# Attention scores as plain float32 products on two row tiles of TensorE, and token mixing through one difference

## The chip, the core and the metric

The kernel runs on one core of a Trainium2 chip. A core has five engines with instruction streams of their own: TensorE (PE in the profile; its weight loads are the row PEld), VectorE (DVE), ScalarE (ACT), GpSimd (POOL) and SyncE (SP, which here only issues DMA transfers). Matrix products are written to PSUM, all else lies in SBUF, and inputs and outputs in HBM. The metric is the device time of one execution in microseconds (us), as the median of several runs.

## The reference

Two layers behind one another: attention with a distance bias over a short local window and a few global keys, then a channel mix ("k" and "r" branches) on its output.

```python
# q, k, v: (4, 8, 768, 64) float32; n_global = 8, n_local = 96
scores = q @ k.T / 8
keep = is_global | is_local            # key < 8, or 0 <= query - key < 96
dist = where(is_global & ~is_local, n_local, abs(query - key))
scores = where(keep, scores - slope[h] * dist, -1e9)
a = exp(scores - max); a = a / (sum(a) + 1e-9)
x = (a @ v), heads side by side        # (4, 768, 512)

x_prev = x shifted by one token, zeros first
xk = mu_k * x + (1 - mu_k) * x_prev
xr = mu_r * x + (1 - mu_r) * x_prev
k = maximum(xk @ w_k, 0)               # (512, 1024)
v = (k * k) @ w_v                      # (1024, 512)
out = sigmoid(xr @ w_r) * v
```

The weights arrive as float64, everything else as float32.

## The kernel before

**Tiles and chunks.** The 4 x 768 tokens are 24 tiles of 128 queries (6 to a batch) and 12 chunks of 256 tokens (two tiles). A tile sees at most 256 keys: 32 from the start of the batch, the 96 before the tile, and its own 128; a batch's first tile (0, 6, 12, 18) has only its own 128.

**Attention of a tile**, for each pair of heads `hp`: `scores` multiplies q and k on PE into one of two PSUM banks `s`; DVE adds the bias (`pat`, or `pat0` for a batch's first tile), takes the row maximum `nmax` and writes `e` (L295); ACT takes exp and the row sum (L296); for every four heads DVE makes the reciprocal `r` (L302, L303) and POOL scales `e` with it (L306). A tile later `transposes` turns `e` on PE (L317) and ACT copies it to `et` (L318); another tile later `weighted` multiplies with `v` into `av` (L334), two heads on two halves of PE's columns, and ACT copies `av` to the chunk's `x` (L345).

**Score products.** A head has 64 rows, PE's array 128. The first `NATIVE` = 7 tiles use plain float32 (L287) with q and k padded by 64 rows of zeros: the two buffers `qz` and `kz` are zeroed once by POOL (L205, L206). From tile 7 on, `load_tile` brings q and k twice, to the upper and the lower 64 partitions, and `split_tile` makes float32r operands of them, that is, rounded values and remainders: `qh` and `kw` by POOL (L196 is the line of its copy helper), `ql` and the lower half of `kw` by DVE (L265, L266), and the keys before the tile by POOL from the previous tile's `kw`. A head is then two float32r products (L289, L290).

**Weights.** Twenty pieces of 128x512 are converted from float64 on the fly during the first tiles: ACT and POOL or DVE shift the exponent (L166 to L170), DVE puts the bits together (L171 to L173), ACT or POOL rounds to the high part (`wk_hi`, `wr_hi`, `wv_hi`, L174 or L196), POOL subtracts to get the low part (`wk_lo`, `wr_lo`, `wv_lo`, L180).

**Channel mix of a chunk**: `mix` makes xk and xr. Of each four column blocks, POOL (for chunk 0 ACT) multiplies x_prev by 1 - mu (L357, L355), DVE adds mu * x (L358), ACT rounds to the high part (L359) and DVE subtracts to get the low part (L360). Then `three` does each product as three float32r products (L371 to L373) into `kp` (first layer), `z` (the gate) and `vps` (second layer); DVE and ACT square `kp` (L397 to L400) and form `sig` (L414), SP stores the result.

**Order.** The loop over 24 steps weaves the pieces: at step n the loads of tile n+1, `weighted` of tile n-2, `transposes` of tile n-1, `scores` of tile n, and between them slices of the channel mix of an earlier chunk (`run_ffn`), and the conversion of weights (`weights_go`). A scheduler then fixes each engine's order before the run; each engine works through its own in order.

Of the kernel before, what the change touches and what calls it, by code (L numbers as in the profile page):

```python
# [24 lines left out]
NATIVE = 7  # first tiles, whose scores are plain float32 products  # L25
# [4 lines left out]
HUGE = (1.875 - 2.0**-13) * 2.0**32  # bits 0x4FEFFC00  # L30
# [3 lines left out]
def tile_biased_attention_channel_mix(ctx: ExitStack, tc: tile.TileContext, qT, kT, v, n_sizes, mu_kr, w_k, w_v, w_r, q_rows, k_rows, v_rows, slopes, out):  # L34
# [33 lines left out]
    kw_pool = fast.enter_context(tc.tile_pool(name="kw", bufs=2))  # L68
    q_pool = fast.enter_context(tc.tile_pool(name="qp", bufs=2))
# [7 lines left out]
    ps_s = fast.enter_context(tc.tile_pool(name="ps_s", bufs=2, space=PSUM))  # L77
# [4 lines left out]
    # the tensor engine's clock rises with use: products of zeros until the first tile is there  # L82
# [7 lines left out]
    # The distance; n_local for a key that is only global, which is over any distance of a local key;  # L90
    # FAR or more where masked: such a key's weight is exactly 0.
# [13 lines left out]
    # 96 keys before the tile, then the tile's own  # L105
# [9 lines left out]
    # tile 0  # L115
# [11 lines left out]
    # later tiles: 32 keys from the start, 96 keys before the tile, the tile  # L127
# [10 lines left out]
    pool.tensor_scalar(mus1, mus, -1.0, 1.0, op0=ALU.mult, op1=ALU.add)  # L138
# [60 lines left out]
    state = {}  # L199
    # the first tiles' queries and keys, with 64 rows of zeros: products of all 128 rows keep the tensor engine's clock up  # L200
    padded = []
    for i in range(2):
        qz = q_pool.tile([128, H, 128], F32, name=f"qz_{i}", tag="qh")
        kz = kw_pool.tile([128, H, 256], F32, name=f"kz_{i}", tag="kw")
        pool.memset(qz[64:128], 0.0)  # L205
        pool.memset(kz[64:128], 0.0)  # L206
        padded.append((qz, kz))

    def load_tile(n):
        b, t = divmod(n, NT)  # L210
        s = state[n] = {}
        native = n < NATIVE
        halves = (0,) if native else (0, 64)
        if native:
            qr, kr = padded[n % 2]
        else:
            qr = p4k.tile([128, H, 128], F32, tag="t4k", name=f"qraw_{n}")
            if n == NATIVE:
                kr = kw_pool.tile([128, H, 256], F32, tag="kw", name=f"kraw_{n}")
            else:  # L220
                kr = p4k.tile([128, H, 128], F32, tag="t4k", name=f"kraw_{n}")
        for o in halves:
            nc.sync.dma_start(qr[o : o + 64], qT[n])
        for o in halves:
            if n <= NATIVE:
                nc.sync.dma_start(kr[o : o + 64, :, 128:256], kT[n])
                if t == 1:
                    nc.sync.dma_start(kr[o : o + 64, :, 0:128], kT[n - 1])
                elif t:
                    nc.sync.dma_start(kr[o : o + 64, :, 0:32], kT[n - t, :, :, 0:32])  # L230
# [11 lines left out]
    def global_v(n):  # L242
        # the tile before, now with the 32 first rows in place of its own
        b, t = divmod(n, NT)
        if t >= 2:
            nc.sync.dma_start(state[n - 1]["va"][0:32], v[b, 0:32, :])

    def split_tile(n):
        t = n % NT
        s = state[n]  # L250
        s["sum"] = s_pool.tile([128, H], F32, name=f"sum_{n}", tag="sum")
        s["nmax"] = s_pool.tile([128, H], F32, name=f"nmax_{n}", tag="nmax")
        s["e"] = {}
# [13 lines left out]
        if t and n > NATIVE:  # L267
            pk = state[n - 1]["kw"]
            if t == 1:
                pool_copy(kw[:, :, 0:128], pk[:, :, 128:256])  # L270
            else:
                pool_copy(kw[:, :, 32:128], pk[:, :, 160:256])
                pool_copy(kw[:, :, 0:32], pk[:, :, 0:32])
        s["qh"], s["ql"], s["kw"] = qh, ql, kw

    def scores(n, hp):
# [5 lines left out]
        ps = ps_s.tile([128, 512], F32, name=f"s_{n}_{hp}", tag="s")  # L282
        for u in range(2):
            h = 2 * hp + u
            o = ps[:, u * 256 : u * 256 + w]
            if n < NATIVE:
                pe.matmul(o, s["qr"][:, h, :], s["kr"][:, h, c0:256], start=True, stop=True)  # L287
            else:
                pe.matmul(o, s["qh"][:, h, :], s["kw"][:, h, c0:256], start=True, stop=False)  # L289
                pe.matmul(o, s["ql"][:, h, :], s["kw"][:, h, c0:256], start=False, stop=True)  # L290
        for u in range(2):
            h = 2 * hp + u
            o = ps[:, u * 256 : u * 256 + w]
            e = e_pool.tile([128, 256], F32, name=f"e_{n}_{h}", tag="e")
            vec.tensor_tensor_reduce(out=e[:, :w], in0=o, in1=p[:, h, :], op0=ALU.add, op1=ALU.min, scale=-0.125, scalar=3.0e38, accum_out=s["nmax"][:, h : h + 1])  # L295
            act.activation(e[:, :w], e[:, :w], AF.Exp, bias=s["nmax"][:, h : h + 1], scale=-1.0, accum_out=s["sum"][:, h : h + 1])  # L296
            s["e"][h] = e
        if hp % 2 == 0:
            return
        h0, nh = 2 * hp - 2, 4  # L300
        r = s_pool.tile([128, nh], F32, name=f"r_{n}_{hp}", tag="r", bufs=8)
# [46 lines left out]
    def mix(xc, xp, tag, tmp_pool, out_pool, on_act=False):  # L348
        m, m1 = mu[tag]
        tmp = tmp_pool.tile([128, 4, 256], F32, name=f"mix_{tag}", tag="t4k")  # L350
        hi = out_pool.tile([128, 4, 256], F32R, name=f"x{tag}_hi", tag=f"x{tag}_hi")
        lo = out_pool.tile([128, 4, 256], F32R, name=f"x{tag}_lo", tag=f"x{tag}_lo")
        for j in range(4):
            if on_act:
                act.activation(tmp[:, j, :], xp[:, j, :], AF.Copy, scale=m1[:, j : j + 1])  # L355
            else:
                pool.tensor_scalar(tmp[:, j, :], xp[:, j, :], m1[:, j : j + 1], 1.0, op0=ALU.mult, op1=ALU.mult)  # L357
            vec.scalar_tensor_tensor(tmp[:, j, :], xc[:, j, :], m[:, j : j + 1], tmp[:, j, :], op0=ALU.mult, op1=ALU.add)  # L358
        act.copy(hi, tmp)  # L359
        vec.tensor_sub(lo, tmp, hi)  # L360
        return hi, lo
# [66 lines left out]
    def run_ffn(amount):  # L428
# [7 lines left out]
        if not queue:  # L436
            budget[0] = 0.0

    load_tile(0)
    split_tile(0)  # L440
    for step in range(NTILES + 1):
        if step + 1 < NTILES:
            load_tile(step + 1)
        if step < NTILES:
            load_v(step)
        for hp in range(4):
# [6 lines left out]
            if step < NTILES:  # L453
                scores(step, hp)
# [7 lines left out]
            if hp == 1 and step + 1 < NTILES:  # L462
                split_tile(step + 1)
# [175 lines left out]
```

## Time and profile before

| | |
|---|---|
| median of 3 runs | 525.86 us (525.65 to 525.88) |
| span of the profiled execution | 524.1 us |
| PE busy | 495.9 us, 95% of the span |
| DVE, ACT, POOL busy | 372.4, 323.6, 283.0 us |
| split of q and k on DVE (L265, L266) | 57.7 us |
| POOL's part of the mixing (L357) | 52.0 us |
| DMA traffic | 48.16 MB |

The span runs from the first to the last instruction of the profiled execution; what lies around it is not in the trace. The profile names an instruction by its line, engine and operation, then by output <- inputs. "x32" is a count. PE's matrix products are pipelined: the durations shown overlap, and the distance from one start to the next is the time that a product costs.

### The profile page before, as it was taken

Reading aid. Unit: us, or ns where it says so; the run is one execution under the profiler, and the core shown is the slowest. Engines: PE = TensorE matmul, PEld = TensorE weight load, DVE = VectorE, ACT = ScalarE, POOL = GpSimd, SP = SyncE. Lnnn points to the kernel's source line nnn. Section 1 sums busy time; section 2 is a strip of 40 time slices with the busy share of each in tenths; the row PEclk is TensorE's granted clock in tenths of the full one; section 3 lists DMA queues with packets and bytes.
Section 4 is the critical chain, followed back from the end, with each engine's and each line's share of the span. In section 5 each row is a group of like instructions: output and inputs, shape, how many; then the busy total and the mean of one; then the engine's idle time right before and its main releaser. Section 6 shows DMA issues by size and latency. Waiting matters only on the chain.

```text
span 524.1 us, 9900 instructions
## 1 busy us (share of the span) xinstructions
PE 495.9 (95%) x3466; PEld 427.2 (82%) x3466; DVE 372.4 (71%) x854; ACT 323.6 (62%) x730; POOL 283.0 (54%) x410
## 2 busy tenths in 40 slices
PE   7885888979999999999999999999999999999995
PEld 4563766869898898898898898898898898898984
DVE  6799999987677766767767867767777865535321
ACT  4868585823957856846847757756757667643220
POOL 8799977987355644544547645535547634203000
PEclk9979799999999999999999999999999999999999
DMA  8998268150350530530521431521422210000101
GB/s 197 322 232 198 67 185 188 41 144 20 107 134 6 141 107 5 157 91 8 162 76 38 130 86 34 133 86 59 124 62 66 62 46 26 35 12 2 41 1 44
DMA packets 27304, 48.16 MB, mean 92 GB/s; under 512 B 7216, under 2 KB 13360, under 8 KB 27248
## 3 DMA queue, kind: packets, MB, share of 16 engines
q1 hardware_dynamic: 27104, 47.46, 34.0%
q8 instruction: 29, 0.48, 0.4%
q14 instruction: 27, 0.22, 0.1%
q10 hardware_dynamic: 144, 0.00, 0.0%
HBM read 41.16 MB, written 6.29 MB: 91 GB/s over the span
## 4 chain that ended last, share of the span: by engine, by line
PE 80%; DVE 11%; POOL 5%; issue 3%; DMA 1%; ACT 0%; DVEq 0%; POOLq 0%
PE vps L372 8%; PE vps L373 8%; PE vps L371 8%; PE kp L371 8%; PE kp L373 8%; PE kp L372 8%; PE av L334 7%; PE t L317 6%; PE z L371 4%; PE z L373 4%; PE z L372 4%; PE s L290 3%; PE s L289 3%; POOL e L306 2%; PE s L287 2%
## 5 line engine op out<-in xcount | busy, mean ns | idle before, releaser
L306 POOL TENSOR_SCALAR e<-e,r 128x256 f32<-128x256 f32 (+1 forms) x192 | 106.1, 570 | 137.0 <-DVE r L303 91.9
L371 PE MATMUL kp<-xk_hi,wk_hi 128*128 128x256 f32 x384 | 108.0, 282 | 0.2 <-DVE kk L398 0.2
L373 PE MATMUL kp<-xk_hi,wk_lo 128*128 128x256 f32 x384 | 107.5, 280 | 0.5 <-POOL wk_lo L180 0.5
L372 PE MATMUL kp<-xk_lo,wk_hi 128*128 128x256 f32 x384 | 107.3, 279 | 0.0
L296 ACT ACTIVATE e<-e,nmax 128x256 f32<-128x256 f32 (+1 forms) x192 | 92.6, 484 | 22.0 <-DVE nmax L295 21.0
L295 DVE CUSTOM_DVE_ANT_0 e<-s,pat 128x256 f32<-128x256 f32 (+1 forms) x192 | 69.0, 395 | 31.0 <-PE s L290 21.2
L372 PE MATMUL vps<-wv_lo,kk_hi 128*128 128x512 f32 x192 | 76.0, 396 | 2.6 <-POOL wv_lo L180 2.6
L371 PE MATMUL vps<-wv_hi,kk_hi 128*128 128x512 f32 x192 | 75.9, 395 | 0.4 <-POOL wv_hi L196 0.4
L373 PE MATMUL vps<-wv_hi,kk_lo 128*128 128x512 f32 x192 | 75.8, 395 | 0.0
L371 PEld LDWEIGHTS kp<-xk_hi,wk_hi 128*128 128x128 f32 x384 | 72.9, 190 | 1.2 <-DVE kk L398 0.6
L373 PEld LDWEIGHTS kp<-xk_hi,wk_lo 128*128 128x128 f32 x384 | 72.8, 190 | 0.9 <-POOL wk_lo L180 0.9
L372 PEld LDWEIGHTS kp<-xk_lo,wk_hi 128*128 128x128 f32 x384 | 72.9, 190 | 0.6
L318 ACT COPY et<-t 128x512 f32<-128x512 f32 (+1 forms) x96 | 52.0, 546 | 20.2 <-PE t L317 19.7
L317 PE MATMUL t<-ident,e 128*128 128x128 f32 x352 | 57.5, 280 | 5.7 <-POOL e L306 5.6
L398 DVE TENSOR_TENSOR kk<-kp,kk 128x512 f32<-128x512 f32 x48 | 33.1, 689 | 41.2 <-ACT kk L397 41.0
L317 PEld LDWEIGHTS t<-ident,e 128*128 128x128 f32 x352 | 41.2, 141 | 19.1 <-POOL e L306 9.2
L334 PE MATMUL av<-et,va 128*64 128x128 f32 x704 | 49.4, 284 | 0.6 <-ACT et L318 0.6
L334 PEld LDWEIGHTS av<-et,va 128*64 128x64 f32 x704 | 40.3, 139 | 10.5 <-issue 5.8
L400 DVE TENSOR_TENSOR kk_lo<-kk,kk_hi 128x512 fp32r<-128x512 f32 x48 | 35.3, 735 | 17.4 <-ACT kk_hi L399 17.3
L399 ACT CAST kk_hi<-kk 128x512 fp32r<-128x512 f32 x48 | 29.8, 622 | 25.6 <-DVE kk L398 25.6
L397 ACT ACTIVATE kk<-kp 128x512 f32<-128x512 f32 x48 | 28.3, 590 | 26.7 <-PE kp L373 24.5
L372 PEld LDWEIGHTS vps<-wv_lo,kk_hi 128*128 128x128 f32 x192 | 36.0, 187 | 10.5 <-POOL wv_lo L180 3.1
(103 smaller groups left out, 1051.1 us busy)
## 6 DMA issues: line engine op xcount, KB each, us to landing
kraw<-in_kT_dram SPq DMA_DIRECT2D x36, 256.0 KB, 3.9
qraw<-in_qT_dram SPq DMA_DIRECT2D x34, 256.0 KB, 4.1
va<-in_v_dram SPq DMA_DIRECT2D x24, 256.0 KB, 3.1
out_dram<-sig SPq DMA_DIRECT2D x24, 256.0 KB, 3.5
w<-in_w_k_dram SPq DMA_DIRECT2D x8, 512.0 KB, 9.1
w<-in_w_v_dram SPq DMA_DIRECT2D x8, 512.0 KB, 3.5
kz<-in_kT_dram SPq DMA_DIRECT2D x8, 256.0 KB, 6.7
w<-in_w_r_dram SPq DMA_DIRECT2D x4, 512.0 KB, 9.3
```

The lines of the kernel that those rows point to most:

```text
L295: vec.tensor_tensor_reduce(out=e[:, :w], in0=o, in1=p[:, h, :], op0=ALU.add, op1=ALU.min, scale=-0.125, scalar=3.0e38, accum_out=s["nmax"] ...
L296: act.activation(e[:, :w], e[:, :w], AF.Exp, bias=s["nmax"][:, h : h + 1], scale=-1.0, accum_out=s["sum"][:, h : h + 1])
L306: pool.tensor_scalar(e[:, :w], e[:, :w], r[:, u : u + 1], 1.0, op0=ALU.mult, op1=ALU.mult)
L317: pe.transpose(pt[:, c : c + 128], e[:, k * 128 : (k + 1) * 128], ident)
L318: act.copy(et[:, : 2 * nb * 128], pt[:, : 2 * nb * 128])
L334: pe.matmul(o, vt[:, h * 64 : (h + 1) * 64], et[:, c : c + 128], start=k == 0, stop=k == nb - 1)
L371: pe.matmul(o, sh, mh, start=first, stop=False)
L372: pe.matmul(o, sh, ml, start=False, stop=False)
L373: pe.matmul(o, sl, mh, start=False, stop=last)
L398: vec.tensor_mul(kk, pv, kk)
L399: act.copy(kkh[:, 2 * fp : 2 * fp + 2, :], kk)
L400: vec.tensor_sub(kkl[:, 2 * fp : 2 * fp + 2, :], kk, kkh[:, 2 * fp : 2 * fp + 2, :])
```

## The change

Two edits go together.

1. **Scores.** The padding, `NATIVE` and `split_tile` go. A tile's q lies in SBUF as 128 partitions: even heads on partitions 0 to 63, odd heads on 64 to 127, four of each side by side; k likewise, with 256 columns a head. `load_tile` brings each half by its own transfer, and copies the keys before the tile from the previous tile's k in SBUF by DMA. `scores` does four heads at once: four plain float32 products of 64 rows, by turns on the upper and the lower row tile of PE's array, which write to two PSUM banks. The score buffer is one of two banks (it was two of one bank). q and k have three buffers each (they had two).
2. **Mixing.** xk = x_prev + mu_k * (x - x_prev), and xr likewise. DVE makes the difference once a chunk (L306 of the new kernel), then adds mu times it to x_prev for both branches (L313). POOL's and ACT's multiplications by 1 - mu go, and `mus1` with them.

```diff
-    kw_pool = fast.enter_context(tc.tile_pool(name="kw", bufs=2))
-    q_pool = fast.enter_context(tc.tile_pool(name="qp", bufs=2))
+    d_pool = fast.enter_context(tc.tile_pool(name="dp", bufs=1))
+    kw_pool = fast.enter_context(tc.tile_pool(name="kw", bufs=3))
+    q_pool = fast.enter_context(tc.tile_pool(name="qp", bufs=3))
...
-    ps_s = fast.enter_context(tc.tile_pool(name="ps_s", bufs=2, space=PSUM))
+    ps_s = fast.enter_context(tc.tile_pool(name="ps_s", bufs=1, space=PSUM))
...
-    for i in range(2):
-        qz = q_pool.tile([128, H, 128], F32, name=f"qz_{i}", tag="qh")
-        kz = kw_pool.tile([128, H, 256], F32, name=f"kz_{i}", tag="kw")
-        pool.memset(qz[64:128], 0.0)
-        pool.memset(kz[64:128], 0.0)
...
     def load_tile(n):
...
+        q = q_pool.tile([128, H // 2, 128], F32, name=f"q_{n}", tag="q")
+        k = kw_pool.tile([128, H // 2, 256], F32, name=f"k_{n}", tag="k")
+        for u in range(2):
+            rows = slice(64 * u, 64 * u + 64)
+            nc.sync.dma_start(q[rows], qT[n].rearrange("d (j u) c -> u d j c", u=2)[u])
+            nc.sync.dma_start(k[rows, :, 128:256], kT[n].rearrange("d (j u) c -> u d j c", u=2)[u])
+
+        if t:
+            before = state[n - 1]["k"]
+            if t == 1:
+                nc.sync.dma_start(k[:, :, 0:128], before[:, :, 128:256])
             else:
+                nc.sync.dma_start(k[:, :, 0:32], before[:, :, 0:32])
+                nc.sync.dma_start(k[:, :, 32:128], before[:, :, 160:256])
...
-    def split_tile(n):
-        pool_copy(qh, s["qr"])
-        pool_copy(cur, kr)
-        vec.tensor_sub(ql, s["qr"], qh)
-        vec.tensor_sub(cur[64:128], kr[64:128], cur[64:128])
...
-                pool_copy(kw[:, :, 32:128], pk[:, :, 160:256])
-                pool_copy(kw[:, :, 0:32], pk[:, :, 0:32])
...
-    def scores(n, hp):
+    def scores(n, half):
...
-                pe.matmul(o, s["qr"][:, h, :], s["kr"][:, h, c0:256], start=True, stop=True)
...
-                pe.matmul(o, s["qh"][:, h, :], s["kw"][:, h, c0:256], start=True, stop=False)
-                pe.matmul(o, s["ql"][:, h, :], s["kw"][:, h, c0:256], start=False, stop=True)
...
+        ps = ps_s.tile([128, 2, 512], F32, name=f"s_{n}_{half}", tag="s")
+        outs = {}
+        for i in range(2):
+            j = 2 * half + i
+            for u in range(2):
+                rows = slice(64 * u, 64 * u + 64)
+                outs[2 * j + u] = o = ps[:, u, i * 256 : i * 256 + w]
+                pe.matmul(o, s["q"][rows, j, :], s["k"][rows, j, c0:256], start=True, stop=True)
...
+    def mix(xc, xp, d_pool, tmp_pool, out_pool):
+
+        d = d_pool.tile([128, 4, 256], F32, name="mix_d", tag="d4k")
+        vec.tensor_sub(d, xc, xp)
...
-                pool.tensor_scalar(tmp[:, j, :], xp[:, j, :], m1[:, j : j + 1], 1.0, op0=ALU.mult, op1=ALU.mult)
-            vec.scalar_tensor_tensor(tmp[:, j, :], xc[:, j, :], m[:, j : j + 1], tmp[:, j, :], op0=ALU.mult, op1=ALU.add)
...
+                vec.scalar_tensor_tensor(tmp[:, j, :], d[:, j, :], mu[tag][:, j : j + 1], xp[:, j, :], op0=ALU.mult, op1=ALU.add)
...
-            if step < NTILES:
-                scores(step, hp)
+            if step < NTILES and hp % 2 == 0:
+                scores(step, hp // 2)
```

What this does to the engines' orders, at three places. The first is PE in the steady stage, at the first scores of tile 14 (`s_14_0`; `t_13_0` are transposes of tile 13, `kp` is the channel mix). Before:

```order
1292 L317 MATMUL t_13_0_3116<-ident_62,e_13_0_2913 128x128 x2
1293 L317 MATMUL t_13_0_3116<-ident_62,e_13_1_2916 128x128 x2
1294 L289 MATMUL s_14_0_3123<-kw_14_3006,qh_14_3004 128x256
1295 L290 MATMUL s_14_0_3123<-kw_14_3006,ql_14_3005 128x256
1296 L289 MATMUL s_14_0_3123<-kw_14_3006,qh_14_3004 128x256
1297 L290 MATMUL s_14_0_3123<-kw_14_3006,ql_14_3005 128x256
1298 L371 MATMUL kp_3083<-xk_hi_2920,wk_hi_70 128x256
```

The same place on PE in the changed kernel:

```order
1180 L272 MATMUL t_13_0_2964<-ident_62,e_13_0_2784 128x128 x2
1181 L272 MATMUL t_13_0_2964<-ident_62,e_13_1_2787 128x128 x2
1182 L249 MATMUL s_14_0_2971<-k_14_2745,q_14_2744 128x256 x4
1183 L327 MATMUL kp_2927<-xk_hi_2806,wk_hi_69 128x256
1184 L328 MATMUL kp_2927<-xk_lo_2807,wk_hi_69 128x256
```

The group holds four heads now, not two, and the next one, `s_14_1`, stands 60 kp and eight transposes later, where the third group of before stood; the second and the fourth place are empty.

The second place is POOL at the end of the weight conversion, between the low parts of the last three pieces (`wa_17` to `wa_19`). Before:

```order
104 L180 TENSOR_TENSOR wv_lo_75<-wa_17_874,wv_hi_74 128x512
105 L306 TENSOR_SCALAR e_6_0_1247<-e_6_0_1247,r_6_1_1305 128x128
106 L306 TENSOR_SCALAR e_6_1_1250<-e_6_1_1250,r_6_1_1305 128x128
107 L306 TENSOR_SCALAR e_6_2_1299<-e_6_2_1299,r_6_1_1305 128x128
108 L306 TENSOR_SCALAR e_6_3_1302<-e_6_3_1302,r_6_1_1305 128x128
109 L196 TENSOR_SCALAR wv_hi_74<-wa_18_939 128x512
110 L357 TENSOR_SCALAR mix_r_1050<-x_1_746,mus1_68 128x256 x4
111 L180 TENSOR_TENSOR wv_lo_75<-wa_18_939,wv_hi_74 128x512
112 L196 TENSOR_SCALAR wv_hi_74<-wa_19_989 128x512
113 L196 TENSOR_SCALAR qh_7_1350<-qraw_7_1206 128x1024
114 L341 MEMSET x_3_1688 128x4
115 L180 TENSOR_TENSOR wv_lo_75<-wa_19_989,wv_hi_74 128x512
```

The same place on POOL in the changed kernel:

```order
94 L178 TENSOR_TENSOR wv_lo_74<-wa_17_876,wv_hi_73 128x512
95 L194 TENSOR_SCALAR wv_hi_73<-wa_18_956 128x512
96 L178 TENSOR_TENSOR wv_lo_74<-wa_18_956,wv_hi_73 128x512
97 L296 MEMSET x_3_1656 128x4
98 L194 TENSOR_SCALAR wv_hi_73<-wa_19_990 128x512
99 L261 TENSOR_SCALAR e_5_4_1133<-e_5_4_1133,r_5_1_1145 128x256
100 L261 TENSOR_SCALAR e_5_5_1136<-e_5_5_1136,r_5_1_1145 128x256
101 L261 TENSOR_SCALAR e_5_6_1139<-e_5_6_1139,r_5_1_1145 128x256
102 L261 TENSOR_SCALAR e_5_7_1142<-e_5_7_1142,r_5_1_1145 128x256
103 L178 TENSOR_TENSOR wv_lo_74<-wa_19_990,wv_hi_73 128x512
```

The mixing `mix_r` and the split `qh_7` are gone from between the weights, the four `e` that stood ahead of piece 18 now stand ahead of the low part of piece 19, and they belong to tile 5, not to tile 6.

The third place is the start of SP's queue. Before:

```order
2 L223 DMA qz_0_177<-in_qT_dram 64x1024
3 L226 DMA kz_0_178<-in_kT_dram 64x8x128
4 L223 DMA qz_1_181<-in_qT_dram 64x1024
5 L226 DMA kz_1_182<-in_kT_dram 64x8x128
6 L228 DMA kz_1_182<-in_kT_dram 64x8x128
7 L239 DMA va_0_192<-in_v_dram 128x512
8 L159 DMA w64_1_211<-in_w_k_dram 128x1024
```

In the changed kernel, from the loads of tile 1 on:

```order
6 L205 DMA q_1_186<-in_qT_dram 64x4x128
7 L206 DMA k_1_187<-in_kT_dram 64x4x128
8 L205 DMA q_1_186<-in_qT_dram 64x4x128
9 L206 DMA k_1_187<-in_kT_dram 64x4x128
10 L211 DMA k_1_187<-k_0_179 128x4x128
11 L226 DMA va_0_195<-in_v_dram 128x512
12 L157 DMA w64_0_221<-in_w_k_dram 128x1024
```

A tile's q and k are four transfers, and the first copy from SBUF to SBUF (row 10), which reads tile 0's k, stands ahead of the first weights.

More of the change, by code (lines that the diff above doesn't have):

```diff
@@ L24 @@
 NCHUNK = NTILES // 2
-NATIVE = 7
 GMAX = 32
@@ new lines, in load_tile @@
+    def load_tile(n):
+        t = n % NT
+        q = q_pool.tile([128, H // 2, 128], F32, name=f"q_{n}", tag="q")
[8 more added lines that the diff above has]
+                nc.sync.dma_start(k[:, :, 0:128], before[:, :, 128:256])
+            else:
+                nc.sync.dma_start(k[:, :, 0:32], before[:, :, 0:32])
+                nc.sync.dma_start(k[:, :, 32:128], before[:, :, 160:256])
+        state[n] = {
+            "q": q,
+            "k": k,
+            "sum": s_pool.tile([128, H], F32, name=f"sum_{n}", tag="sum"),
+            "nmax": s_pool.tile([128, H], F32, name=f"nmax_{n}", tag="nmax"),
+            "e": {},
+        }
@@ L281, in scores @@
         p = pat if t else pat0
[L282 to L293, printed above, removed]
+        ps = ps_s.tile([128, 2, 512], F32, name=f"s_{n}_{half}", tag="s")
[6 more added lines that the diff above has]
+                pe.matmul(o, s["q"][rows, j, :], s["k"][rows, j, c0:256], start=True, stop=True)
+        h0, nh = 4 * half, 4
+        for h in range(h0, h0 + nh):
             e = e_pool.tile([128, 256], F32, name=f"e_{n}_{h}", tag="e")
-            vec.tensor_tensor_reduce(out=e[:, :w], in0=o, in1=p[:, h, :], op0=ALU.add, op1=ALU.min, scale=-0.125, scalar=3.0e38, accum_out=s["nmax"][:, h : h + 1])
+            vec.tensor_tensor_reduce(out=e[:, :w], in0=outs[h], in1=p[:, h, :], op0=ALU.add, op1=ALU.min, scale=-0.125, scalar=3.0e38, accum_out=s["nmax"][:, h : h + 1])
             act.activation(e[:, :w], e[:, :w], AF.Exp, bias=s["nmax"][:, h : h + 1], scale=-1.0, accum_out=s["sum"][:, h : h + 1])
             s["e"][h] = e
[L298 to L301, printed above, removed]
+        r = s_pool.tile([128, nh], F32, name=f"r_{n}_{half}", tag="r", bufs=8)
         vec.tensor_scalar(r, s["sum"][:, h0 : h0 + nh], 1.0e-9, None, op0=ALU.add)
@@ L345, in weighted @@
             act.copy(xt[:, :, 1 + 128 * i : 129 + 128 * i], s["av"].rearrange("p (a q) -> p a q", a=4))
[L348 to L357, printed above, removed]
[L358 to L361 removed]
+    def mix(xc, xp, d_pool, tmp_pool, out_pool):
+        d = d_pool.tile([128, 4, 256], F32, name="mix_d", tag="d4k")
+        vec.tensor_sub(d, xc, xp)
+        parts = []
+        for tag in "kr":
+            tmp = tmp_pool.tile([128, 4, 256], F32, name=f"mix_{tag}", tag="t4k")
+            hi = out_pool.tile([128, 4, 256], F32R, name=f"x{tag}_hi", tag=f"x{tag}_hi")
+            lo = out_pool.tile([128, 4, 256], F32R, name=f"x{tag}_lo", tag=f"x{tag}_lo")
+            for j in range(4):
+                vec.scalar_tensor_tensor(tmp[:, j, :], d[:, j, :], mu[tag][:, j : j + 1], xp[:, j, :], op0=ALU.mult, op1=ALU.add)
+            act.copy(hi, tmp)
+            vec.tensor_sub(lo, tmp, hi)
+            parts.append((hi, lo))
+        return parts
     def channel_mix(xk, xr, out_rows, f_pool, f2_pool, ps_f):
```

59 lines of the change are left out of this document (3 added, 56 removed).

## The prediction

> **What bounds the kernel now.** I read the page's shares and slices first, then the busy time by stretches, then the waits, then single rows.
>
> ```profile
> span 524.1 us, 9900 instructions
> PE 495.9 (95%) x3466; PEld 427.2 (82%) x3466; DVE 372.4 (71%) x854; ACT 323.6 (62%) x730; POOL 283.0 (54%) x410
> PE   7885888979999999999999999999999999999995
> PE 80%; DVE 11%; POOL 5%; issue 3%; DMA 1%; ACT 0%; DVEq 0%; POOLq 0%
> ```
> ```profile
> 60.00:115.00 55.00, 47.72 (x317) 39.21 (x316) 52.53 (x102) 32.55 (x80) 46.20 (x51) 0.99 0.48 128
> 115.00:300.00 185.00, 185.00 (x1347) 163.83 (x1346) 136.97 (x305) 124.80 (x271) 100.34 (x151) 1.00 0.32 88
> 300.00:515.00 215.00, 215.00 (x1568) 191.08 (x1567) 130.29 (x288) 125.07 (x265) 83.36 (x137) 1.00 0.19 54
> ```
> The columns behind the length are PE, PEld, DVE, ACT, POOL busy, then the granted clock. From 115 us on PE is busy every microsecond at full clock, so there each PE microsecond counts one to one and all that DVE, ACT, POOL and DMA do is covered. Before that, DVE (52.5 of 55 us) sets the pace with POOL. The chain of waits shows where the one stage passes into the other:
>
> ```profile
> 106.03 3.10 POOL mix_r L357 x4
> ...
> 112.35 2.19 POOL wv_lo L180
> 114.58 0.50 PE vps L372
> ```
> The last weight part to be converted frees PE at 114.58 us; behind it nothing is waited for but PE itself. So the sum has two terms: PE work behind that point, and the date of that point.
>
> **Term 1: PE work of the scores behind 115 us.** A steady stretch of PE, by start time:
>
> ```profile
> 302.44 0.28 PE L373 MATMUL kp<-xk_hi,wk_lo 128*128 128x256 f32 x1
> 302.65 2.02 PE L334 MATMUL av<-et,va 128*64 128x128 f32 x32
> 304.60 0.66 PE L317 MATMUL t<-ident,e 128*128 128x128 f32 x4
> 305.01 0.36 PE L289 MATMUL s<-kw,qh 128*128 128x256 f32 x1
> 305.21 0.28 PE L290 MATMUL s<-kw,ql 128*128 128x256 f32 x1
> 305.33 0.28 PE L289 MATMUL s<-kw,qh 128*128 128x256 f32 x1
> ...
> 305.57 0.28 PE L371 MATMUL kp<-xk_hi,wk_hi 128*128 128x256 f32 x1
> ```
> Durations overlap, so I use distances between starts: a float32r score product takes 0.12 us (305.21 to 305.33). A pair of heads has four, 0.48 us; four heads, which the new kernel does in one go, 0.95 us.
>
> The plain float32 product stands in the first tiles:
>
> ```profile
> 65.83 1.03 PE L287 MATMUL s<-kz,qz 128*128 128x256 f32 x4
> 66.79 1.15 PE L334 MATMUL av<-et,va 128*64 128x128 f32 x16
> 67.86 1.13 PE L287 MATMUL s<-kz,qz 128*128 128x256 f32 x4
> 68.92 0.66 PE L334 MATMUL av<-et,va 128*64 128x128 f32 x8
> ```
> ```profile
> 116.51 1.52 PE L334 MATMUL av<-et,va 128*64 128x128 f32 x22
> 117.96 0.39 PE L371 MATMUL kp<-xk_hi,wk_hi 128*128 128x256 f32 x1
> 118.19 0.28 PE L372 MATMUL kp<-xk_lo,wk_hi 128*128 128x256 f32 x1
> ```
> One such product leaves two records. Three prices come out of these rows:
> - Drain: between the last kp and av lie 0.21 us (302.44 to 302.65) where 0.12 is usual: 0.09 us whenever PE passes from 128x128 products to products on part of the array.
> - Record: the four records at 65.83 reach the av in 0.96 us with one drain: (0.96 - 0.09) / 4 = 0.217 us for 256 columns, 0.108 for 128.
> - Exposed weight load: the group at 67.86, just behind an av, takes 1.06 us, 0.10 more; the first kp behind an av takes 0.23 (117.96 to 118.19), 0.11 more.
>
> Do part-array products overlap? The 32 av records have 128 columns each and write two halves of the columns by turns. One after another they would need 32 x 0.108 = 3.5 us; they took 1.95 (302.65 to 304.60), drain and loads included. So two column tiles run side by side. The row tiles of the change are not in this trace; I take them to behave like these.
>
> New half of a tile (four heads, four products, eight records on two row tiles): drain 0.09, load 0.10, four steps of 0.217 = 0.87, drain 0.09, load of the next product 0.11: **1.26 us against 0.95**, so +0.30 us. Bounds: with no drain and no exposed load 0.87 (-0.08); with no overlap 0.39 + 8 x 0.217 = 2.13 (+1.18).
>
> ```profile
> L289 PE MATMUL s<-kw,qh 128*128 128x256 f32 x120 | 36.1, 323 | 0.0
> L289 PE MATMUL s<-kw,qh 128*128 128x128 f32 x16 | 4.2, 290 | 0.0
> ```
> L289 is run once a head: 120 / 4 = 30 halves of 256 columns and 16 / 4 = 4 of 128 (a batch's first tile: 0.39 + 4 x 0.108 = 0.82, taken 0.1 below before). Term 1: 30 x 0.30 - 4 x 0.1 = **+8.6 us**; bounds -4 (30 x -0.08, 4 x -0.5) and +37.
>
> The Trainium skill ("TensorEngine Tiling (Array Packing)", Key Properties) says that a change of the tiling mode drains the engine; the trace agrees, with the 0.09 us above. "TensorE: Matmul & The Clock Gate" (Part 3, Measured speedup vs the span model) prices tiles run together as one duration plus about 4 ns for each further tile and has no drain: by it alone a half would come near the 0.87 us of the lower bound, which is the second rival below. No run here shows row tiles yet.
>
> **Term 2: the stretch up to 114.6 us.** It is DVE and POOL work, so halving the plain float32 scores of tiles 0 to 6 on PE gains nothing of itself. What changes on the chain:
>
> ```profile
> 5.56 1.94 POOL L206 MEMSET kz<- 64x2048 f32 x1
> ...
> 111.26 1.05 POOL L196 TENSOR_SCALAR qh<-qraw 128x1024 fp32r<-128x1024 f32 x1
> ```
> ```profile
> 5.36 0.40 DVE L117 TENSOR_SCALAR btmp<-btmp,sizes 128x128 f32<-128x128 f32 x1
> 5.68 1.89 DVE L128 TENSOR_SCALAR btmp<-btmp,sizes 128x96 f32<-128x96 f32 x1
> ```
> - The zero fills go. DVE's L128 ends at 5.68 + 1.89 = 7.57, when the last fill (to 7.50) lets go; its larger neighbour L117 took 0.40. That is -1.5 us for the bias and all behind it.
> - On POOL, mix_r (3.10) and qh (1.05) no longer stand ahead of the last weight part, but the new order puts the four e of tile 5's second half there:
>
> ```profile
> 100.78 3.10 POOL L306 TENSOR_SCALAR e<-e,r 128x128 f32<-128x128 f32 x4
> L360 DVE TENSOR_TENSOR xk_lo<-mix_k,xk_hi 128x1024 fp32r<-128x1024 f32 x12 | 14.7, 1226 | 0.8 <-ACT xk_hi L359 0.8
> ```
>   Four small ones took 3.10, so -1.0 us net.
> - DVE gets one subtraction of 128x1024 a chunk, priced by xk_lo at 1.2 us; chunks 0 and 1 fall here: +2.4 us. ACT's eight products of chunk 0 go; ACT is not on the chain.
> - Less POOL work beside DVE (fills, mixing, splits) may shorten stretched DVE instructions: 0 to -6 us, the size of the mixing and fills removed; I take -1.
>
> Sum -1.1 us; range +4 (the SP copies below) to -8.
>
> Covered by PE's 100%: the splits on POOL and DVE, later mixing, and the single score buffer. PE may not write a half's scores until DVE has read the four heads before:
>
> ```profile
> L295 DVE CUSTOM_DVE_ANT_0 e<-s,pat 128x256 f32<-128x256 f32 x160 | 60.9, 417 | 27.9 <-PE s L290 19.2 <-POOL mix_k L357 4.5 <-PE s L287 2.3
> ```
> Four heads are 1.7 us; two halves lie at least 60 kp (7 us) apart on PE. Without that cover a half would cost up to 1.7 us more.
>
> DMA: per tile q and k come in four pieces, and the keys before come by one or two copies from the previous tile's SBUF, in short pieces, on SP's queue behind the loads. Nearest rows:
>
> ```profile
> kz<-in_kT_dram SPq DMA_DIRECT2D x4, 192.0 KB, 8.5
> kz<-in_kT_dram SPq DMA_DIRECT2D x4, 64.0 KB, 9.7
> qraw<-in_qT_dram SPq DMA_DIRECT2D x34, 256.0 KB, 4.1
> ```
> In the steady stage the DMA share is 0.19 to 0.32, the loads stand half a tile step (some 9 us) ahead of use: cost 0, at worst a wait on SP. At the start, weights queue behind the first copy, which must wait for tile 0's keys; that is the +4 end.
>
> **Sum**, against the profiled span of 524.1 us (1.8 below the median of 525.86, which I carry along): 525.9 + 8.6 - 1.1 = **533.4 us**.
>
> **Rivals.**
> 1. *The start gains more* (ends faster). In the first 115 us PE waits:
>
> ```profile
> PE s L287 <- DVE nmax L295: 6.8, 3, 3.2
> PE t L317 <- POOL e L306: 5.6, 10, 1.2
> PE vps L372 <- POOL wv_lo L180: 2.6, 2, 1.8
> ```
>   The place is the last wv_lo at 112.35. It decides once that part lands 9 us sooner, by about 105 us; with a shift of 12 us the time is 525.9 + 8.6 - 12 = 522.5. For it: 15 us of waits are there, POOL loses some 11 us of work. Against it: DVE loses none, and is 96% busy. Chance 0.11.
> 2. *Row tiles drain nothing.* Term 1 at its lower bound: 525.9 - 4 - 1.1 = 521. Against: the av rows. Chance 0.07.
> 3. *Two heads are not done at once* (the change doesn't do what it says): +37 - 1 = 562. Against: the column tiles overlap. Chance 0.10.
> 4. *Late keys*: the copies hold SP's queue and PE waits at each tile's first scores, 0.5 us by 15 tiles: 541. For it: 9.7 us landings; against: those were with DMA at 0.89. Chance 0.08.
>
> **How the numbers follow.** My forecast has 0.64. From 521 to 546 lie it, both faster rivals mostly, and late keys; outside are the serial case and the far ends of the start. This kernel's measurement can tell some 0.2% (1 us) from no change. Faster: rivals 1 and 2 and the forecast's low tail, 0.18; same 0.07; slower 0.75.
>
> **What would show it.** Right: score records at 0.217 steps in twos that start almost together, 0.09 us gaps on both sides, PE at 100% from about 113 us, and some 0.6 us more per tile step. Wrong: records one after another (rival 3); kp right behind the scores with no gap (rival 2); a last wv_lo before 105 us (rival 1); waits of s for DMA (rival 4), or of s for DVE's nmax behind 115 us, which would make the single score buffer the cost.

## The result, and the profile after

| | before | after |
|---|---|---|
| median | 525.87 us (525.65 to 526.99, 4 runs) | 541.54 us (541.25 to 541.78, 4 runs) |
| span of the profiled execution | 524.1 us | 539.7 us |

The changed kernel is slower: ratio 1.0297, 95% interval 1.0282 to 1.0313, which is 15.7 us. The forecast was 533.4 us.

The page of the changed kernel, its shares, slices and chain by engine:

```profile
span 539.7 us, 9670 instructions
PE 508.8 (94%) x3466; PEld 419.8 (78%) x3466; DVE 306.5 (57%) x832; ACT 306.6 (57%) x710; POOL 166.9 (31%) x257
PE   7765878999999999999999999999999999999995
PEclk9885697999999999999999999999999999999999
PE 78%; DVE 14%; POOL 2%; DMA 2%; issue 2%; ACT 1%; POOLq 0%; DVEq 0%; ACTq 0%; SPq 0%
```

The three helpers lost 200 us of work between them (DVE 66, POOL 116, ACT 17), and PE gained 13. From 115 us on PE is the engine that counts, and what the helpers lose does not show there. The busy time by stretches (PE, PEld, DVE, ACT, POOL, then the granted clock, that is, the share of its full clock that the profile says PE was given):

```profile
15.00:60.00 45.00, 30.83 (x172) 19.22 (x172) 42.74 (x97) 28.97 (x81) 35.60 (x42) 0.73 1.00 233
60.00:115.00 55.00, 48.66 (x306) 40.05 (x307) 51.86 (x105) 33.50 (x72) 37.89 (x40) 0.88 0.37 108
115.00:300.00 185.00, 184.52 (x1324) 156.01 (x1323) 95.41 (x287) 114.21 (x262) 42.47 (x77) 1.00 0.24 67
300.00:515.00 215.00, 215.00 (x1542) 183.64 (x1541) 104.11 (x288) 120.23 (x271) 43.72 (x76) 1.00 0.16 48
```

From 116 us on it is the old picture: PE is never idle. New are the first 115 us: the granted clock is 0.73 and 0.88 there. Before the change:

```profile
15.00:60.00 45.00, 33.12 (x192) 23.28 (x192) 42.58 (x111) 34.09 (x93) 40.95 (x47) 0.87 0.89 211
```

and 0.99 from 60 to 115 us. What PE waited for (us in total, times, longest), the waits that the prediction named:

```profile
PE s L249 <- DVE nmax L253: 9.4, 4, 4.8
PE s L249 <- DMA k<-k: 1.4, 1, 1.4
PE s L249 <- DMA k<-in_kT_dram: 0.3, 1, 0.3
```

All of these lie before 115 us. The chain of waits, where the early stage passes into the late one:

```profile
111.78 2.80 POOL e L261 x4
114.58 1.27 POOL wv_lo L178
115.85 0.04 issue
115.90 0.50 PE vps L328
```

The last weight part frees PE at 115.90 us, where it was 114.58.

**Where the 15.6 us of span are.** To split the span I use one instruction group that both kernels have, the weighted sum `av`, whose groups begin once per tile. Tile 6's begins here, before and after:

```profile
148.36 0.88 PE L334 MATMUL av<-et,va 128*64 128x128 f32 x12
```
```profile
152.38 0.88 PE L289 MATMUL av<-et,va 128*64 128x128 f32 x12
```

So 4.0 us are lost ahead of it, the early part. Behind it lie 524.1 - 148.4 = 375.7 us before and 539.7 - 152.4 = 387.3 us after, 11.6 us more, the late part. It is perfectly regular. Two `av` groups six tiles (one batch) apart, tiles 12 and 18, before:

```profile
245.43 2.02 PE L334 MATMUL av<-et,va 128*64 128x128 f32 x32
...
361.39 2.02 PE L334 MATMUL av<-et,va 128*64 128x128 f32 x32
```

and after:

```profile
252.79 2.02 PE L289 MATMUL av<-et,va 128*64 128x128 f32 x32
...
372.72 2.02 PE L289 MATMUL av<-et,va 128*64 128x128 f32 x32
```

A batch costs 115.96 us before and 119.93 after: +3.97. Two halves of a tile in the changed kernel, by start time:

```profile
303.00 0.60 PE L272 MATMUL t<-ident,e 128*128 128x128 f32 x4
303.53 1.13 PE L249 MATMUL s<-k,q 64*128 64x256 f32 x8
...
314.18 0.66 PE L272 MATMUL t<-ident,e 128*128 128x128 f32 x4
314.76 1.13 PE L249 MATMUL s<-k,q 64*128 64x256 f32 x8
315.83 0.39 PE L327 MATMUL kp<-xk_hi,wk_hi 128*128 128x256 f32 x1
316.06 0.28 PE L328 MATMUL kp<-xk_lo,wk_hi 128*128 128x256 f32 x1
...
319.35 0.28 PE L329 MATMUL kp<-xk_hi,wk_lo 128*128 128x256 f32 x1
```

Eight score records take 1.07 us with the drain behind them, so the two row tiles do run side by side (in the trace the two records of a pair start 7 ns apart, and the pairs 0.216 us). Behind them the first `kp` takes 0.23 us, 0.11 more than usual, and ahead of them four `t`, 0.109 us each, need 0.53 us (303.00 to 303.53), 0.09 more. All three are the prices of the forecast.

Not forecast is the rest of those rows: 28 steps of `kp` from 316.06 to 319.35 are 117.5 ns each. Before the change the 29 steps that follow 305.57 (its row stands in the prediction) end here, at 113.4 ns each:

```profile
308.86 0.28 PE L373 MATMUL kp<-xk_hi,wk_lo 128*128 128x256 f32 x1
```

The same product has two paces, and the change moves it to the slower one. Counted over the distances between neighbouring `kp` behind 115 us, before has 636 fast ones (113 to 114 ns) and 350 slow ones (some 118); after has none below 115 ns.

### The profile page after: what moved, and what is told of

Read it like the earlier page. It is cut to its first block, busy times and chain, and to the rows that moved or that the text cites. A ratio compares the mean times of both kernels' runs of the same rounds, so it can differ in the third digit from the quotient of the medians.

```text
span 539.7 us, 9670 instructions
## 1 busy us (share of the span) xinstructions
PE 508.8 (94%) x3466; PEld 419.8 (78%) x3466; DVE 306.5 (57%) x832; ACT 306.6 (57%) x710; POOL 166.9 (31%) x257
## 4 chain that ended last, share of the span: by engine, by line
PE 78%; DVE 14%; POOL 2%; DMA 2%; issue 2%; ACT 1%; POOLq 0%; DVEq 0%; ACTq 0%; SPq 0%
PE kp L327 8%; PE vps L327 8%; PE vps L328 8%; PE vps L329 8%; PE kp L329 8%; PE kp L328 8%; PE s L249 7%; PE av L289 6%; PE t L272 6%; PE z L327 4%; PE z L328 4%; PE z L329 4%; DVE wa L170 2%; DVE wa L171 2%; DVE e L253 2%
## 5 line engine op out<-in xcount | busy, mean ns | idle before, releaser
L261 POOL TENSOR_SCALAR e<-e,r 128x256 f32<-128x256 f32 (+1 forms) x192 | 112.1, 601 | 247.8 <-ACT et L273 84.7
L327 PE MATMUL kp<-xk_hi,wk_hi 128*128 128x256 f32 x384 | 111.8, 292 | 1.7 <-ACT xk_hi L314 1.7
L253 DVE CUSTOM_DVE_ANT_0 e<-s,pat 128x256 f32<-128x256 f32 (+1 forms) x192 | 65.7, 396 | 35.0 <-PE s L249 33.9
L327 PE MATMUL vps<-wv_hi,kk_hi 128*128 128x512 f32 x192 | 78.5, 410 | 0.0
L249 PE MATMUL s<-k,q 64*128 64x256 f32 (+1 forms) x384 | 59.2, 422 | 11.1 <-DVE nmax L253 9.4
L272 PE MATMUL t<-ident,e 128*128 128x128 f32 x352 | 60.9, 292 | 4.4 <-POOL e L261 3.3
L289 PE MATMUL av<-et,va 128*64 128x128 f32 x704 | 51.6, 293 | 6.3 <-ACT et L273 6.3
L249 PEld LDWEIGHTS s<-k,q 64*128 64x128 f32 x384 | 36.7, 207 | 24.2 <-DVE nmax L253 10.9
L289 PEld LDWEIGHTS av<-et,va 128*64 128x64 f32 x704 | 42.2, 144 | 15.9 <-ACT et L273 7.2
L300 ACT COPY x<-av 128x512 f32<-128x512 f32 x24 | 14.1, 586 | 55.0 <-PE av L289 55.0
```

The lines of the kernel that those rows point to most:

```text
L249: pe.matmul(o, s["q"][rows, j, :], s["k"][rows, j, c0:256], start=True, stop=True)
L253: vec.tensor_tensor_reduce(out=e[:, :w], in0=outs[h], in1=p[:, h, :], op0=ALU.add, op1=ALU.min, scale=-0.125, scalar=3.0e38, accum_out=s[" ...
L261: pool.tensor_scalar(e[:, :w], e[:, :w], r[:, u : u + 1], 1.0, op0=ALU.mult, op1=ALU.mult)
L272: pe.transpose(pt[:, c : c + 128], e[:, k * 128 : (k + 1) * 128], ident)
L289: pe.matmul(o, vt[:, h * 64 : (h + 1) * 64], et[:, c : c + 128], start=k == 0, stop=k == nb - 1)
L327: pe.matmul(o, sh, mh, start=first, stop=False)
```

## The experiments

Times are medians of four runs (t_twice five); the kernel before ran beside them on the same chip, at 525.7 to 526.7 us. The theory that I set out with: the early stage, the switches of the score halves and the pace of `kp` each carry a part, and all three come from the scores. The rivals: the mixing carries the early part, or the kind of scores does not touch the pace.

### One part of the change at a time

**scores_only**: the changed kernel with the old mixing.

```diff
...
-        xk, xr = mix(xt[:, :, 1:257], xt[:, :, 0:256], d_pool, p4k, f_pool)
+        xk = mix(xt[:, :, 1:257], xt[:, :, 0:256], "k", p4k, f_pool, c == 0)
+        xr = mix(xt[:, :, 1:257], xt[:, :, 0:256], "r", p4k, f_pool, c == 0)
...
```

> The changed kernel with the mixing of before (POOL and ACT multiply x_prev by 1 - mu, no difference on DVE). Theory A: of the 15.7 us that the change costs, some 9 are mode changes of the new score halves behind 115 us, some 3 a slower pace of the kp products there (117.8 instead of 113.3 ns from start to start), and some 3.5 the stretch up to 115 us, all three from the scores; then this kernel takes 541.5 us, within 1.5. Rival B: the 3.5 us of the early stretch come from the mixing (a difference more on DVE, another order on POOL); then 538 us.

Measured 539.23 us, between the two and within neither: the scores carry 13 of the 15.7 us, the mixing 2.3 in this company.

**hyb_late**: the new scores only from tile 7 on, the old mixing.

```diff
...
+        rowtiles = n >= NATIVE
...
```

> The kernel before, with its padded float32 scores in tiles 0 to 6 and its mixing; from tile 7 on the scores of the change (four heads at once, plain float32 on two row tiles, keys before the tile copied by DMA). Theory A: 525.9 + 9 + 3 = 537.9 us, within 1.5, with kp at 117.8 ns throughout. If the pace of kp does not hang on the kind of the scores: 535. If the early stretch costs nothing of itself and all lies behind tile 7: 541.5.

Measured 536.74 us, ratio 1.0202 (1.0184 to 1.0220), +10.7. The batch of six tiles takes 119.83 us, as in the changed kernel, and tile 6's `av` begins at 147.9, as before the change: the late loss stands alone here, and is the larger part. 830 of its `kp` distances are slow and 136 fast.

**hyb_early**: the new scores only in tiles 0 to 6.

```diff
...
+        rowtiles = n < NATIVE
...
```

> The other half: tiles 0 to 6 with the scores of the change, from tile 7 on the float32r scores of before, mixing of before. Theory A: 525.9 + 3.5 = 529.4 us, within 1.5, with some 35 us at half clock before 115 us (14 in the kernel before). Rival B or a steady stage that carries all: 526, within 1.

Measured 530.56 us, +4.6, with the old 115.96 us for a batch and 639 fast `kp`. Its tile 6 `av` begins at 152.1, 3.8 us late. So rival B falls for the scores' share: the early loss comes with the scores too. Early and late add up to 15.3 us, scores_only has 13.2; the early part is not strictly additive.

**mix_only**: the kernel before with the new mixing alone.

```diff
...
+        for i in range(2):
+            d = d_pool.tile([128, 2, 256], F32, name="mix_d", tag="d4k")
+            vec.tensor_sub(d, xc[:, 2 * i : 2 * i + 2, :], xp[:, 2 * i : 2 * i + 2, :])
...
```

> The kernel before with the mixing of the change alone (for want of room the difference is made in two halves of 128x512, and the zeros of the start lie in a buffer that is used later). If the mixing costs nothing while the early scores are padded (late_mix against hyb_late: -0.7 us): 525.2, within 0.8. If it costs the 2.3 us of the changed kernel against scores_only by itself: 528.2.

Measured 531.64 us, +5.9: more than either said. The batch takes 116.32 us, and of the 636 fast `kp` 372 are left (631 are slow), so some 1 us is pace; the rest is ahead of tile 6, where PE now waits 11.3 us for POOL's `e` instead of 5.6:

```profile
PE t L316 <- POOL e L305: 11.3, 13, 3.6
```

**late_mix**: hyb_late with the new mixing, that is, the whole change but for tiles 0 to 6.

```diff
...
-        xk = mix(xt[:, :, 1:257], xt[:, :, 0:256], "k", p4k, f_pool, c == 0)
-        xr = mix(xt[:, :, 1:257], xt[:, :, 0:256], "r", p4k, f_pool, c == 0)
+        xk, xr = mix(xt[:, :, 1:257], xt[:, :, 0:256], d_pool, p4k, f_pool)
...
```

> The whole change from tile 7 on and its mixing, but tiles 0 to 6 with the padded float32 scores of before; this is hyb_late with the mixing of the change. If the mixing costs its 2.3 us (541.5 less 539.2 of scores_only) wherever it stands: 536.7 + 2.3 = 539. If it costs only while thin early scores hold PE back: 536.7, within 0.8.

Measured 536.05 us: here the mixing costs nothing. Its price is then +2.3, +5.9 and -0.7 us in three surroundings. It moves DVE and POOL work in the crowded first 115 us, and what comes of that hangs on the order it falls into. I have no price for it that would carry over. mix_only also makes its difference in two halves, so it is not quite the mixing of the change.

### The prices per passage, and the pace

**s_first**: the changed kernel with the scores ahead of the transposes.

```diff
-            if step:
-                transposes(step - 1, hp)
             if step < NTILES and hp % 2 == 0:
                 scores(step, hp // 2)
+            if step:
+                transposes(step - 1, hp)
```

> The changed kernel with a half's scores ahead of the transposes in the program, so that PE goes av, s, t, kp instead of av, t, s, kp. If the prices per passage hold (drain 0.09, exposed load 0.11): the drain of t to s and the load of kp go, t's first load of 0.05 comes, -0.15 us at a tile's first half and some -0.05 at the second, 19 tiles behind 115 us: -3.8, so 537.7 us within 1. If each passage of s costs the same wherever it stands: 541.5.

Measured 539.34 us, -2.2. The batch takes 118.46 us, 1.47 less, that is 0.245 us a tile where 0.20 was expected: the passages have about these prices. Ahead of tile 6 it loses 1.8 us, which hides part of the gain, and the time misses the 537.7 expected. **late_s_first** clears that up: the same order from tile 7 on only, in late_mix.

```diff
+            if step < NTILES and step >= NATIVE:
+                scores(step, hp)
             if step:
                 transposes(step - 1, hp)
-            if step < NTILES:
+            if step < NTILES and step < NATIVE:
                 scores(step, hp)
```

> late_mix (536.05 us) with the scores ahead of the transposes from tile 7 on. By the steady stage of s_first (118.46 us for six tiles, 119.93 in the changed kernel, so 0.245 us a tile) times 17 tiles: -4.2, so 531.9 within 0.8. If the gain of s_first came from the early tiles: 536.

Measured 532.04 us. Behind tile 6's `av` it takes 4.0 us less than late_mix: the gain that s_first measured for a tile carries over.

**swap**: the kernel before with the scores ahead of the transposes.

```diff
-            if step:
-                transposes(step - 1, hp)
             if step < NTILES:
                 scores(step, hp)
+            if step:
+                transposes(step - 1, hp)
```

> The kernel before with the scores of a pair ahead of the transposes in the program, so that kp follows t and not s. If the faster pace of kp (113.3 ns in 636 of its products, 117.8 in the others) hangs on the float32r scores standing right ahead of it: all kp at 117.8, +2.9 us, 528.8. If it hangs on something else: 525.9, within 0.8, with some 600 kp at 113.3.

Measured 533.08 us, +7.4. Fast `kp` fall from 636 to 51, and a batch takes 117.10 us, 1.14 more: the pace does hang on the order just ahead of `kp`, with nothing else changed in the late stage. That makes some 3 us behind tile 6; 4 more were lost ahead of it (its `av` begins at 152.3), which I had not expected.

### The early stage

**thin64**: the kernel before, with products of 64 rows in tiles 0 to 6.

```diff
-                pe.matmul(o, s["qr"][:, h, :], s["kr"][:, h, c0:256], start=True, stop=True)
+                pe.matmul(o, s["qr"][0:64, h, :], s["kr"][0:64, h, c0:256], start=True, stop=True)
```

> The kernel before, only that the products of tiles 0 to 6 use the 64 rows of q and k without the 64 rows of zeros (which are still filled). Same instructions, half the rows. If rows that are used keep the clock up: clearly more than 14 us at half clock before 115 us, and 1 to 3.5 us more than 525.9. If the clock follows only how long PE is busy: the same half-clock stretches and 525.9, within 1.

Measured 530.96 us, +5.0. The first stretches by windows, of the kernel before and then of thin64:

```profile
15.00:35.00 20.00, 15.96 (x98) 10.41 (x98) 17.93 (x53) 15.81 (x47) 17.25 (x21) 0.90 1.11 291
```
```profile
15.00:35.00 20.00, 19.96 (x66) 11.78 (x65) 13.40 (x44) 13.58 (x42) 14.09 (x19) 0.50 1.07 280
35.00:60.00 25.00, 22.74 (x102) 15.13 (x101) 24.56 (x64) 19.59 (x51) 24.74 (x26) 0.64 0.63 141
```

PE is busy for all of these 20 us and stays at half clock all the same; DVE, which set the pace before, falls from 17.93 to 13.40 us of work there. So the zeros under q and k were worth 5 us: without them the clock did not come up for 20 us. It came up later, and the rows of thin64 show where:

```profile
36.59 1.97 PE L317 MATMUL t<-ident,e 128*128 128x128 f32 x8
38.49 1.11 PE L334 MATMUL av<-et,va 128*64 128x128 f32 x8
39.53 0.66 PE L317 MATMUL t<-ident,e 128*128 128x128 f32 x4
```

Three microseconds without a score product stand ahead of the first full-speed row (four `t` in 0.66 us). The Trainium skill ("TensorE: Matmul & The Clock Gate", Part 1) puts the clock down to how busy the engine has recently been, and lets it rise after some 3.4 us of sustained work. By that alone these 20 us would have run at full clock; the measurement decides, and it says that something in which the padded and the bare product differ counts too. They differ in the rows in use, and in that 64 rows run on one row tile of the array; the two were not tried apart.

**late_thin**: the same one-line edit, made in late_mix.

> late_mix (536.05 us), only that the products of tiles 0 to 6 use the 64 rows of q and k without the 64 rows of zeros. Same instructions otherwise. If the clock at half speed, brought on by fewer rows in use, is what the changed kernel loses before 115 us: over 35 us at half clock (20 in late_mix) and about 5 us more, 541 within 1.5, as much as the changed kernel itself. If the changed kernel loses them by its order, its one score buffer or its copies: 536, within 0.8.

Measured 546.75 us, +10.7, twice what was expected. Its granted clock reads 1.00 in these stretches:

```profile
15.00:35.00 20.00, 19.97 (x72) 12.18 (x71) 14.39 (x41) 13.59 (x40) 13.98 (x20) 1.00 1.06 280
```

but its steps do not bear that out. Late_thin and then late_mix, by start time:

```profile
30.16 2.07 PE L285 MATMUL s<-kz,qz 64*128 64x256 f32 x4
32.17 2.03 PE L330 MATMUL av<-et,va 128*64 128x128 f32 x16
34.12 2.07 PE L285 MATMUL s<-kz,qz 64*128 64x256 f32 x4
```
```profile
25.44 1.03 PE L285 MATMUL s<-kz,qz 128*128 128x256 f32 x4
26.40 0.66 PE L330 MATMUL av<-et,va 128*64 128x128 f32 x8
```

Four score records take 2.01 us instead of 0.96: half speed. So the granted clock of late_thin cannot be used. For the other kernels it gives an estimate of the time at half speed between 15 and 115 us, if the clock is either full or half: 14 us before (0.93), 38 after the change (0.81), 48 in thin64 (0.76), 14 in late_mix (0.93). Some of the expectations count it off the length of the steps instead, which comes out some us lower or higher.

In the changed kernel itself two score products run side by side, but for half as long, and PE stands idle between them:

```profile
43.27 2.08 PE L249 MATMUL s<-k,q 64*128 64x256 f32 x8 [4.76 <-DVE nmax L253]
46.09 1.14 PE L272 MATMUL t<-ident,e 128*128 128x128 f32 x4 [0.74 <-POOL e L261]
...
51.46 1.22 PE L249 MATMUL s<-k,q 64*128 64x256 f32 x2 [2.47 <-DVE nmax L253]
52.61 3.73 PE L289 MATMUL av<-et,va 128*64 128x128 f32 x32
56.27 1.12 PE L272 MATMUL t<-ident,e 128*128 128x128 f32 x4
```

Here four heads wait 4.76 us for the one score buffer, and then all runs at half speed (2.08 for 1.13, 1.14 for 0.60, 3.73 for 2.02). Is the clock then the loss? Two kernels add full products to keep it up.

**warm**: four products of zeros ahead of each half's scores in tiles 0 to 6.

```diff
+        if n < 7:
+            for i in range(4):
+                pe.matmul(ps[:, i % 2, :], zeros[:, 0:128], zeros, start=True, stop=True)
```

> The changed kernel; for tiles 0 to 6 four products of zeros (bf16, 128x128 by 512 columns) go to the two score banks just ahead of each half's scores, which overwrite them. If the loss before 115 us comes from the clock at half speed (37 us of it, 14 before the change): less than 20 us at half clock, and 3 to 4.6 us less than the 541.5 us of the changed kernel, so 537 to 538.5. If the order of the work, the single score buffer or the copies lose it and the clock only shows it: 541.5 or more, since the filling costs PE 14 x 0.85 us.

Measured 543.84 us, +2.3. Half speed fell from 38 to some 24 us (granted clock 0.88), but the time did not follow.

**t_twice**: each transpose of tiles 0 to 6 done twice.

```diff
-                pe.transpose(pt[:, c : c + 128], e[:, k * 128 : (k + 1) * 128], ident)
+                for _ in range(2 if n < 7 else 1):
+                    pe.transpose(pt[:, c : c + 128], e[:, k * 128 : (k + 1) * 128], ident)
```

> The changed kernel with each transpose of tiles 0 to 6 done twice into the same columns: more full products on PE beside the thin scores, some 1.7 us of PE a tile at full speed, without a new wait. If half speed before 115 us (33 us by the length of the steps, 18 in the kernel before) is what the changed kernel loses there: under 20 us at half speed and some 3 us less, 538.5. If its order of work loses it: 541.5 or up to 5 us more, since PE has 14 us of idle time before 115 us that the 12 us of copies may or may not find.

Measured 543.56 us, +2.0. (Its profiled execution took 547.66 us, so nothing is read from its trace.) In warm, 14 us less at half speed are worth 7 us of PE, and the filling costs 14 x 0.85 = 12 us of PE at full speed, of which the idle time takes up only a part: up to tile 6's `av` PE is busy 132.1 us, 4.8 more than in the changed kernel (127.3). By that balance a clock that is bought with extra work does not pay. The zeros under the old scores took no time of PE beside bare products of 64 rows: four records show 1.13 us with them (67.86 in the kernel before) and 1.13 without (66.08 in late_thin, at full speed).

**pad_four**: late_mix with tiles 0 to 6 scored in the order of the change, four heads at once into one buffer.

```diff
-        if rowtiles and hp % 2:
+        if hp % 2:
             return
-        heads = range(2 * hp, 2 * hp + (4 if rowtiles else 2))
+        heads = range(2 * hp, 2 * hp + 4)
...
```

> late_mix (536.05 us) with tiles 0 to 6 scored in the order of the change: four heads at once into two banks that DVE must have read before the next four; products padded to 128 rows as in late_mix. If the rows in use (by the clock) make the difference between late_mix and the changed kernel: 536, within 1. If four heads at once do: 541, within 1.5, with PE waiting 9 us for DVE's nmax as in the changed kernel (4 in late_mix).

Measured 538.32 us, +2.3 (tile 6's `av` at 149.34 instead of 147.55). The order alone loses some 2 of the 5.5 us that lie between late_mix and the changed kernel. The larger rest came with the products and their operands on two row tiles; how much of it is the clock and how much the four loads and the copies of keys was not tried apart.

**Busy or idle.** One more reading tells the kernels apart. Up to tile 6's `av` the four kernels below run the same number of products on PE (758 or 759 records). These are the stretches of the kernel before, thin64, late_mix and the changed kernel; the number behind the length is PE's busy time, the rest is idle:

```profile
0.00:148.36 148.36, 125.80 (x758) 98.70 (x758) 129.40 (x312) 94.52 (x237) 118.50 (x147) 0.95 0.62 157
```
```profile
0.00:154.98 154.98, 140.49 (x758) 107.33 (x758) 128.14 (x311) 92.05 (x231) 118.84 (x145) 0.81 0.56 145
```
```profile
0.00:147.55 147.55, 126.62 (x759) 98.16 (x759) 119.61 (x313) 92.05 (x229) 103.80 (x125) 0.93 0.55 145
```
```profile
0.00:152.38 152.38, 127.28 (x759) 95.83 (x759) 123.01 (x313) 92.53 (x229) 88.88 (x121) 0.88 0.56 145
```

thin64 is busy 14.7 us longer than the kernel before and idle 8.1 less (its profiled execution took 532.38 us, 1.4 above its median): PE itself became the slow engine. The changed kernel is busy 1.5 us longer than the kernel before (0.7 longer than late_mix) and idle 2.5 us more (4.2 more than late_mix). So its early loss shows mostly as waiting: 9.4 us for `nmax` (6.8 before), and 6.3 us of `av` for ACT's `et` (0.6 before), 4.4 of them in one piece up to 82.53. ACT has two conversions of weights ahead of that `et` and waits 1.92 and 1.41 us for the transfers of these weights. Up to 115 us it waits 11.4 us for weights, 1.0 before and 2.1 in late_mix. The first weight goes out on SP's queue, behind the new loads and the first copy, at 9.41 us (5.08 before). Why the later ones come late is not shown: mix_only waits 7.1 us for them with the old loads. On the chain up to the last weight part PE stands, from 20 us on, with one piece of 1.16 us (the four `t` at 46.09), in late_thin with over 37 us. That half speed made PE late in thin64 is shown; that it is what the changed kernel lost its time by is not.

## Why the prediction came out as it did

**Right: the mechanism and the price of the late stage.** PE stays the bound; row tiles overlap; a half costs 0.09 + 0.10 + 0.87 + 0.09 + 0.11 us. Behind tile 6's `av` stand the scores of tiles 8 to 23: 28 halves of 256 columns and four of 128. At +0.30 and -0.1 they make 8.0 us; measured are 11.6 less 2.9 for the pace, 8.7. The rivals are out, and that late keys named 541 us is a coincidence: the start gained nothing, nothing runs serially, no passage is free, and PE waits for keys for 1.4 and 0.3 us, all early. The span rule of the Trainium skill ("TensorE: Matmul & The Clock Gate", Part 3, Measured speedup vs the span model) leaves out the 0.09 us of drain on either side that the rows show here.

**Missed: the pace of `kp`.** Term 1 priced the neighbours of the scores, with one record of `kp` each, and put everything farther off at nothing, as unchanged. 636 distances got 4.5 ns longer: 2.9 us. The rows were there to be seen: in the profile before, 305.57 to 305.91 (three steps) and 301.14 to 302.44 (eleven) show both paces.

**Wrong: term 2.** It said -1.1 us, with a range up to +4; measured is 4.0 us more at tile 6, 5.1 us off. With the 2.9 us of pace that is the whole miss. Two steps failed:

- "The date of that point" was to stand for the whole early stage. It moved by +1.3 us (115.90 for 114.58), and the other 2.7 us are PE work carried past it: up to tile 6's `av` 20 records of `t` stand behind it, 8 before, and four more each of `s` and `av`. hyb_early shows best that the date does not decide: its last weight part ends at 109.6 us, 4.9 earlier than before (114.5), and its tile 6 comes 3.8 us later.
- "Halving the plain float32 scores of tiles 0 to 6 on PE gains nothing of itself" asked what the padding costs, not what it keeps up. thin64 shows what that was worth in the kernel before, 5.0 us. The granted clock of 0.87 from 15 to 60 us was in the profile, a comment in the kernel above the zero fills says that they are there for the clock, and no rival said that it could fall. In the changed kernel PE is busy no less than before, although its scores were halved, while the granted clock went from 0.87 to 0.73 and from 0.99 to 0.88.

The weights behind the first copy were named, as the +4 end of the range, and they do come later; how much of the 4.0 us they carry is open. The gain at the start came as sized (DVE's instruction of 1.89 us beside the fills, L128, takes 0.27 now, as L127), but nothing of it is left at tile 6.

In part wrong too: the single score buffer was put at no cost, as covered by PE. That holds behind 115 us, where PE never waits for `nmax`; before it, PE waits 9.4 us for it (6.8 before the change), and pad_four prices the order of four heads at some 2 us.

The difference on DVE was sized rightly, 1.21 us each for two chunks, but says little, as mix_only and late_mix show.

**Open**: some 2 us of the early loss go with the order of four heads at once (pad_four); the rest is not split between the clock, the later weights and the copies of keys. Why `kp` has two paces is not known.

No kernel run here is faster than the one before the change. The best with the new scores in the late stage is late_s_first, 532.04 us.

## What to carry to other kernels

A change that makes PE's products thinner in a stage where PE is not the bound can still cost time, through the clock, as thin64 and late_thin show: look at the granted clock of the stage, and ask what keeps it there. Padding to full rows took no time here beside bare products of 64 rows, and is worth trying before any filling with extra products. Then split the stage into busy and idle time of PE: a slow clock shows as busy time, and where the idle time grew, look for who came late. Where PE is the bound, price each passage between shapes from distances between starts, and then compare the pace of the bulk products too, since 4.5 ns on 636 of them weighed as much as ten score halves.

## What the runs showed of the hardware that I had not expected

- Two steady paces of one and the same 256-column float32r product, 113.3 and 117.8 ns, chosen at the start of a run of them and kept to its end. In the kernel before, all 18 runs behind float32r scores of 256 columns are fast and all ten behind `vps` slow; behind the short scores four are fast and two slow, behind transposes two fast and one slow. So the row ahead alone does not settle it, but swap, which changed that row, left 51 fast distances of 636.
- Plain float32 products of 64 rows, mixed with transposes and weighted sums, left the clock at half, even with PE busy for 19.96 of 20 us (thin64); padded to 128 rows they had 0.90 with 15.96 us busy.
- The granted clock in a profile can be wrong over a long stretch: 1.00 from 15 to 35 us in late_thin, where the steps are twice their length.
